# Batch 0 of a fused attention and MLP kernel: a cast split over three engines, W1 pieces paired, a token tile interleaved earlier

## The chip, the cores and the metric

The kernel runs on one core of one Trainium2 chip. The metric is the device time of one execution in microseconds (us), as a median over runs; smaller is better. The core has a matrix engine (TensorE, PE in the profile; its weight loads are listed apart as PEld), a vector engine (VectorE, DVE), a scalar engine for activation functions (ScalarE, ACT), a general engine (GpSimd, POOL) and a queue engine (SyncE, SP). Each runs its own instructions in program order and waits for the others through semaphores. Transfers are issued from the queues of SP, ACT and POOL.

## What is computed

```
x: 8 batches x 8 heads x 512 tokens x 64;  state: 8 x 8 x 32 x 64;  w_in: 512 x 2048;  w_out: 2048 x 512
a     = softmax(x @ state^T / 8)      xread = a @ state      (512 rows per batch)
a2    = softmax(state @ x^T / 8)      sread = a2 @ x         (32 rows per batch)
rows  = [xread, sread] with the 8 heads side by side -> 4352 x 512
out   = silu(rows @ w_in) @ w_out                             (float32)
```

## The kernel before

The kernel never forms xread. For each batch b it multiplies the state by w_in first, which gives a matrix W1 of (8 heads x 32 states) by 2048, held as two groups of 128 rows (`hg` 0 and 1). The hidden layer of the 512 tokens is then silu(aT^T @ W1), where aT is the transposed softmax. The work of a batch is cut as follows.

- A **W1 piece** is 512 columns of W1 of one batch: `w1_mms` (L449) issues 8 matmuls into two PSUM banks, and `w1_out` (L471) copies one bank on DVE and one on ACT into SBUF (`both`, L196). `w1_cols` does both at once. A batch has four pieces.
- A **hidden tile** ft is 128 of the 2048 hidden columns: `emit_G1` (L523) issues two `h` matmuls (one per head group) into one of two PSUM banks of the pool psH and a Silu on ACT (L546) into `g`. `upto(k)` (L592) issues hidden tiles in order until k are done.
- A **step** `G2(b, tt, ft)` (L548) is one `o` matmul: hidden tile ft, token tile tt of 128 tokens, accumulated in an output bank (`o` or `o_a`). Batch 0 has four output banks, o0, o1, a0, a1, for tt = 0 to 3.
- `store` (L564) copies an output bank to SBUF and issues the store on SP.

The attention of a batch is a chain: `cast_x` (L127) turns x into bf16, `pe_transpose_x` (L243) transposes it on PE and copies it out, `scores` (L297) and `exps` (L312) give the exponentials, `norm` (L369) reduces, takes the reciprocal and multiplies (head group 0 on POOL, 1 on DVE), and the result is transposed back (`pe_transpose_a`, L393, as `aT`). ACT loads a function table whenever it goes from Silu to Exp and back; the one-element activations on `warm` (L608, L657, L676) place those loads.

The order on each engine is the order of the program, which is written out by hand. PSUM has eight banks: o0, o1 (psO), two h banks (psH) and a0 to a3 (psA); `bank` hands out the psA banks in turn from the list `banks`. The start of batch 0 (L258 to L270 and L597 to L632) runs its attention chain with x arriving in two transfers, one per head group. In the second head group ACT casts token chunks 2 and 3 and POOL chunks 0 and 1 (L268, L269). Matmuls on zeros (`keep_busy`, L161) fill gaps. W1 of batch 0 starts with 128 and then 384 columns.

The loop L643 goes over hidden tiles 0 to 13 of batch 0: `upto` keeps two to four hidden tiles ahead (LEAD0), at ft = 2, 6, 10 a further W1 piece of batch 0 is made, at ft = 5 and 9 pieces 0 and 1 of batch 1, all in banks a2 and a3; at ft = 4 the state row of batch 1 is transposed, at ft = 11 x of batch 1 is cast, at ft = 12 it is transposed. The fourth token tile (tt = 3) takes part in steps 0 to 2 only. Its steps 3 to 5 come at ft = 12, its steps 6 to 11 while the softmax of batch 1 is on its way, and 12 to 15 after that (L685 to L702), together with pieces 2 and 3 of batch 1. From L704 on, batches 1 to 7 follow in one loop.

Of the kernel before, what the change touches and what calls it, by code (L numbers as in the profile page):

```python
# [9 lines left out]
BF16 = mybir.dt.bfloat16  # L10
# [4 lines left out]
EXP = mybir.ActivationFunctionType.Exp  # L15
# [26 lines left out]
def kernel(  # L42
# [84 lines left out]
    def cast_x(b, eng, c0=0, nc_=4, h0=0, nh=H):  # L127
        if b < 2:
            x_nat[b] = padded(b)
        elif b not in x_nat:  # L130
            x_nat[b] = xpool.tile([128, 4, 4, 128], BF16, tag="x_nat", name=f"x_nat{b}")
        copy(
            eng,
            x_nat[b][:, ds(c0, nc_), ds(h0 // 2, nh // 2), :].rearrange(
                "p c k (u d) -> p c k u d", u=2
            ),
            x_f[b % 2][:, ds(h0, nh), ds(c0, nc_), :].rearrange("p (k u) c d -> p c k u d", u=2),
        )
# [12 lines left out]
    def load_w_out(g0, n):  # L151
        nc.gpsimd.dma_start(w_out_sb[:, ds(g0, n), :], wout_re[:, ds(g0, n), :])

    def copy(eng, dst, src):
        if eng is nc.scalar:
            nc.scalar.activation(dst, src, func=COPY, bias=0.0)  # L156
        else:
            eng.tensor_copy(dst, src)  # L158


    def keep_busy(n, pool, tag):  # L161
        ps = pool.tile([128, 512], FP32, tag=tag, name="ps_busy")
        for _ in range(n):
            nc.tensor.matmul(  # L164
                ps[:], busy[:, 0:128], busy[:], start=True, stop=True, skip_group_check=True
            )
# [50 lines left out]
    def place_one_state(b, ps, eng):  # L217
        for u in range(2):
            by_n = slots_of(b)[u].rearrange("p g (k m v) -> p g k m v", m=16, v=2)
            for v in range(2):  # L220
                copy(eng, by_n[:, :, 0:3:2, :, v], ps[ds(64 * v, 64), :, :, u, :])
# [21 lines left out]
    def pe_transpose_x(b, hg, nb=2, new=bank, engs=(nc.vector, nc.scalar), only=None):  # L243
        if b not in xT:
            xT[b] = xtpool.tile([128, 4, 4, 128], BF16, tag="xT", name=f"xT{b}")
        m = 4 // nb
        for u in range(nb) if only is None else only:
            ps = new([128, m, 2, 128], BF16, "ps_xt")
            for i in range(m):
                for j in range(2):  # L250
                    nc.tensor.transpose(  # L251
                        ps[:, i, j, :],
                        x_nat[b][:, m * u + i, 2 * hg + j, :],
                        ident[:],
                    )
            copy(engs[u], xT[b][:, ds(m * u, m), ds(2 * hg, 2), :], ps[:])
# [9 lines left out]
    o_tags = ["o0", "o1"]  # L266
    new_o = lambda sh, dt, nm: psO.tile(sh, dt, tag=o_tags.pop(), name=nm)
    cast_x(0, nc.scalar, 2, 2, 4, 4)  # L268
    cast_x(0, nc.gpsimd, 0, 2, 4, 4)  # L269
    pe_transpose_x(0, 0, 2, new_o, (nc.vector, nc.vector))  # L270

    st_x = pers.tile([128, 8, B, 4, 2, 2], BF16)

# [116 lines left out]
            aT[b][:, hg, :, :], an[b, hg][:].rearrange("p c s n -> p (c s n)")  # L390
        )

    def pe_transpose_a(b, hg, eng, new=bank, c0=0, n=4):  # L393
        ps = new([128, n, 128], BF16, "ps_at")
        for c in range(n):
            nc.tensor.transpose(ps[:, c, :], an[b, hg][:, c0 + c, :, :], ident[:])
        copy(eng, aT[b][:, hg, ds(c0, n), :], ps[:])


    xm_ps = {}  # L400
# [48 lines left out]
    def w1_mms(b, cols, new=bank):  # L449
        pss = {}  # L450
        if b not in W1:
            W1[b] = wpool.tile([128, 2, DF], BF16, tag="W1", name="W1")
        for f, n in cols:
            for hg in range(2):
                pss[f, hg] = new([128, 512], FP32, "ps_w1")
            for s in range(4):
                for hg in range(2):
                    h = HEAD_OF_SLOT[hg][s]
                    r = 64 * (h % 2)
                    nc.tensor.matmul(  # L460
                        pss[f, hg][ds(32 * s, 32), 0:n],
                        stT[ds(r, 64), b, h // 2, s % 2, :],
                        w_in_sb[ds(r, 64), h // 2, ds(f, n)],
                        start=True,
                        stop=True,
                        tile_position=(r, 32 * s),
                        skip_group_check=True,
                    )
        return pss

    def w1_out(b, cols, engs, pss, at=0):  # L471
        for f, n in cols:
            for hg in range(2):
                copy(engs[hg], W1[b][:, hg, ds(f + at, n)], pss[f, hg][:, ds(at, n)])

    def w1_cols(b, cols, engs, new=bank):
        w1_out(b, cols, engs, w1_mms(b, cols, new))

    def w1_chunks(b, fbs, engs):
        w1_cols(b, [(512 * fb, 512) for fb in fbs], engs)  # L480
# [111 lines left out]
    def upto(k):  # L592
        while done[0] < min(k, (B + 1) * NFT):
            emit_G1(done[0])
            done[0] += 1

    new_h = lambda sh, dt, nm: psH.tile(sh, dt, tag="h1", name=nm)  # L597
    keep_busy(1, psH, "h1")
    scores(0, 0)
    exps(0, 0)  # L600
    keep_busy(1, psH, "h1")
    pe_transpose_x(0, 1, 2, new_h, (nc.vector, nc.scalar))
    norm(0, 0)
    scores(0, 1, 2)
    exps(0, 1)
    norm(0, 1, ((nc.vector, 0, 4),), 2)
    pss0 = w1_mms(0, [(0, 128)])
    nc.scalar.activation(warm[:], busy[:, 0:1], func=SILU, bias=0.0)  # L608
    w1_out(0, [(0, 128)], (nc.scalar, nc.scalar), pss0)
    load_w_in(1024)  # L610
    load_w_out(8, 4)
    load_w_in(1536)
    for hg in range(2):
        load_x(1, 4 * hg, 4)
    load_w_out(12, 4)
    load_states()
    load_x(2)
    for i in range(3):
        ones_beside_x(i, nc.gpsimd)
    keep_busy(3, psH, "h1")  # L620
    pss0 = w1_mms(0, [(128, 384)])
    keep_busy(2, psH, "h1")
    new_o = lambda sh, dt, nm: psO.tile(sh, dt, tag=o_tags.pop(), name=nm)
    o_tags[:] = ["o0", "o1"]
    for c in (0, 2):
        pe_transpose_a(0, 0, nc.scalar, new_o, c, 2)
    for c in (0, 2):
        pe_transpose_a(0, 1, nc.vector, bank, c, 2)
    upto(1)
    w1_out(0, [(128, 128)], (nc.vector, nc.vector), pss0)  # L630
    w1_out(0, [(128, 256)], (nc.vector, nc.vector), pss0, 128)
    upto(2)  # L632

    banks[:] = ["a2", "a3"]
    turn[0] = 0
    W0 = {2: (512, 512), 6: (1024, 512), 10: (1536, 512)}
    LEAD0 = [2, 2, 2, 2, 2, 3, 2, 3, 3, 2, 2, 4, 4]  # L640
    F3 = 3
    ready = 4
    for ft in range(NFT - 2):  # L643
        upto(min(ft + LEAD0[min(ft, 12)], ready))
        if ft in W0:
            w1_cols(0, [W0[ft]], both)
            ready = sum(W0[ft]) // 128
        if ft == 4:
            place_one_state(1, transpose_one_state(st1_n), nc.vector)
        if ft in (5, 9):  # L650
            w1_chunks(1, ({5: 0, 9: 1}[ft],), both)
        if ft == 11:
            for hg in range(2):
                cast_x(1, nc.vector, 0, 4, 4 * hg, 4)
            load_x(3)
        if ft == 12:
            nc.scalar.activation(warm[:], busy[:, 0:1], func=EXP, bias=0.0)  # L657
            for i in range(F3, F3 + 3):
                G2(0, 3, i)
            pe_transpose_x(1, 0, 1, engs=(nc.vector,))  # L660
            pe_transpose_x(1, 1, 1, engs=(nc.vector,))
        for tt in range(4 if ft < F3 else 3):
            G2(0, tt, ft)
    F3 += 3
    banks[:] = ["a2", "a3", "a0", "a1"]
    turn[0] = 0
    scores(1, 0, new=new_h)
    scores(1, 1, new=new_h)
    exps(1, 0)
    exps(1, 1)  # L670
    for tt in (0, 2, 1):
        G2(0, tt, 14)
        G2(0, tt, 15)
        if tt != 1:
            store(0, tt, nc.scalar)
    nc.scalar.activation(warm[:], busy[:, 0:1], func=SILU, bias=0.0)  # L676
    norm(1, 0)
    norm(1, 1, ((nc.vector, 0, 4),))
    tail_tags = ["a2", "a3", "a0", "o0"]

    def tail_bank(shape, dtype, name):
        tag = tail_tags.pop(0)
        return (psO if tag == "o0" else psA).tile(shape, dtype, tag=tag, name=name)

    for ft in range(F3, NFT):  # L685
        if ft == 12:
            pe_transpose_a(1, 0, nc.vector, new_h)
        if ft == 14:
            pe_transpose_a(1, 1, nc.vector, new_h)
            store(0, 1, nc.vector)  # L690
            cols = [(1024, 512), (1536, 512)]
            pss1 = w1_mms(1, cols, tail_bank)
            w1_out(1, cols, (nc.vector, nc.vector), pss1)
            for i in (2, 3):
                for c in range(4):
                    cast_x(i, nc.gpsimd, c, 1)
            transpose_states()
            transpose_x(2)
            upto(NFT + 2)
        G2(0, 3, ft)  # L700
    upto(NFT + 3)
    store(0, 3, nc.vector)  # L702

# [100 lines left out]
```

The softmax here doesn't subtract the row's maximum and nothing guards it: scores larger than these inputs give would overflow.

## Time and profile before

| | us |
|---|---|
| median of 4 runs (lowest, highest) | 216.42 (216.29, 216.45) |
| the profiled execution | 216.29 |
| its span, first to last instruction | 214.5 |
| PE busy in it | 206.0 |
| ACT busy | 139.5 |
| DVE busy | 76.6 |
| POOL busy | 39.4 |

How to read it: the profile is of one execution, whose own time is 1.8 us more than its span. Times inside it are counted from the start of the span. Busy time of PE counts each matmul from its start to its modelled end, and matmuls overlap, so PE is shown busy where it only drains. What tells of idle time on PE is the distance from one start to the next: 0.216 us between matmuls of 512 columns. A few matmul records are missing in a trace, which shows as one distance of about twice that length. In a row of the timeline the number after x is how many instructions were merged into it.

### The profile page before, as it was taken

The numbers are of one execution on the slowest core, as the hardware profiler recorded it, in microseconds if no ns is written. First come the engines' busy times: TensorE is split into PE (matmuls) and PEld (weight loads), VectorE is DVE, ScalarE is ACT, GpSimd is POOL, SyncE is SP. The second block draws the span as 40 slices with busy tenths as digits, with TensorE's granted clock in tenths as the row PEclk, the third lists the DMA queues.
The fourth block names the chain that finished last, engine by engine and source line by source line (L and its number), as shares of the span: only waits on it lengthen the run. The fifth ranks groups of instructions, "written<-read, shape, count | busy, mean of one in ns | idle before, by whom it ended". The sixth has DMA issues, their size and how long they took to land.

```text
span 214.5 us, 3867 instructions
## 1 busy us (share of the span) xinstructions
PE 206.0 (96%) x1549; PEld 96.9 (45%) x1575; DVE 76.6 (36%) x170; ACT 139.5 (65%) x244; POOL 39.4 (18%) x61
## 2 busy tenths in 40 slices
PE   7899999999899999999999999999999999999993
PEld 2443344445344444444444444444444444466653
DVE  3733247855951156106610651135312415200011
ACT  3866577699557876699459956886675366644410
POOL 8683013702420222004110402000200000000000
PEclk9999999999999999999999999999999999999999
DMA  6999999795649447464657395114310211011112
GB/s 185 203 205 207 291 268 349 178 236 205 93 101 271 145 107 196 95 201 105 174 74 244 75 158 121 49 52 104 96 51 18 89 49 53 0 49 49 52 49 98
DMA packets 42914, 28.66 MB, mean 134 GB/s; under 512 B 28048, under 2 KB 37776, under 8 KB 42896
## 3 DMA queue, kind: packets, MB, share of 16 engines
q1 hardware_dynamic: 36720, 20.65, 36.8%
q0 software_dynamic: 5888, 7.64, 17.1%
q8 instruction: 12, 0.20, 0.4%
q10 hardware_dynamic: 288, 0.13, 0.2%
q14 instruction: 6, 0.05, 0.1%
HBM read 17.43 MB, written 8.91 MB: 123 GB/s over the span
## 4 chain that ended last, share of the span: by engine, by line
PE 88%; DVE 5%; ACT 3%; issue 1%; POOL 0%; POOLq 0%
PE o L555 47%; PE h L514 25%; PE ps_w L460 4%; PE h L535 3%; PE o_a L555 2%; PE ps_busy L164 2%; PE o_part L577 2%; DVE W L158 2%; ACT exp_nat L317 1%; DVE rs L376 1%; PE ps_xt L251 1%; PE ps_sr L412 1%; DVE rc L428 1%; PE ps_scT L329 1%; ACT L317 1%
## 5 line engine op out<-in xcount | busy, mean ns | idle before, releaser
L555 PE MATMUL o<-w_out_sb,g 128*128 128x512 bf16 x483 | 129.3, 379 | 1.8 <-issue 1.1
L546 ACT ACTIVATE g<-h 128x512 bf16<-128x512 f32 (+1 forms) x143 | 81.4, 573 | 37.0 <-PE h L514 23.0
L555 PEld LDWEIGHTS <-g 128*128 128x128 bf16 x528 | 50.0, 98 | 57.6 <-issue 3.2
L514 PE MATMUL h<-aT,W 128*128 128x512 bf16 x242 | 72.2, 379 | 0.5 <-ACT g L546 0.3
L158 DVE COPY o_sb<-o 128x512 f32<-128x512 f32 x15 | 10.4, 691 | 89.1 <-PE o L555 85.1
L514 PEld LDWEIGHTS <-W 128*128 128x128 bf16 x254 | 24.5, 98 | 31.8 <-issue 2.0
L158 DVE CAST W<-ps_w 128x512 bf16<-128x512 f32 (+2 forms) x37 | 23.0, 649 | 25.3 <-PE ps_w L460 25.3
L156 ACT ACTIVATE W<-ps_w 128x512 bf16<-128x512 f32 (+1 forms) x31 | 16.4, 570 | 12.6 <-PE ps_w L460 12.6
L158 POOL CAST x_nat<-x_f 128x512 bf16<-128x512 f32 x24 | 14.5, 647 | 33.1 <-issue 22.2
L156 ACT ACTIVATE o_sb<-o 128x512 f32<-128x512 f32 x16 | 9.6, 597 | 12.1 <-PE o L555 8.9
L359 POOL TENSOR_TENSOR an<-e,rcn 128x512 bf16<-128x512 bf16 x5 | 7.6, 1517 | 49.6 <-DVE rcn L357 49.6
L460 PE MATMUL ps_w<-w_in_sb,stT 64*32 64x512 bf16 (+2 forms) x264 | 11.1, 375 | 0.7 <-DVE W L158 0.7
L555 PE MATMUL o_a<-w_out_sb,g 128*128 128x512 bf16 x32 | 10.2, 379 | 0.1
L535 PE MATMUL h<-xmT,w_in_sb 128*128 128x256 bf16 x64 | 9.6, 272 | 0.0
L535 PEld LDWEIGHTS <-w_in_sb 128*128 128x128 bf16 x64 | 6.3, 98 | 3.9
L164 PE MATMUL ps_busy<-busy 128*128 128x512 bf16 x15 | 6.2, 523 | 1.2 <-DVE warm L171 1.2
L460 PEld LDWEIGHTS <-stT 64*32 64x32 bf16 x264 | 3.4, 89 | 7.4 <-issue 4.9
L748 ACT ACT_TABLE_LOAD x5 | 6.4, 1283 | 0.1
L343 ACT ACTIVATE eT<-ps_scT 128x512 bf16<-128x512 f32 x10 | 5.4, 594 | 1.6 <-PE ps_scT L329 1.6
L379 POOL TENSOR_TENSOR an<-exp_nat,rc 128x512 bf16<-128x512 bf16 x3 | 3.1, 1047 | 18.0 <-ACT eT L343 10.7
L356 DVE TENSOR_REDUCE rs<-e 128x32 f32<-128x1024 bf16 x5 | 6.1, 1212 | 0.2 <-DMA e<-eT 0.2
L108 POOL DMA_DIRECT2D x_f<-in_x_dram x4 | 3.3, 845 | 11.7 <-DVE x_rows L158 9.4
(76 smaller groups left out, 104.3 us busy)
## 6 DMA issues: line engine op xcount, KB each, us to landing
out_dram<-o_sb SPq DMA_DIRECT2D x33, 256.0 KB, 2.4
x_f<-in_x_dram SPq DMA_DIRECT2D x4, 1024.0 KB, 6.1
x_f<-in_x_dram POOLq DMA_DIRECT2D x2, 1024.0 KB, 12.7
w_in_sb<-in_moe_w_in_dram POOLq DMA_DIRECT2D x3, 512.0 KB, 10.1
w_out_sb<-in_moe_w_out_dram POOLq DMA_DIRECT2D x3, 512.0 KB, 11.9
x_f<-in_x_dram SPq DMA_DIRECT2D x2, 512.0 KB, 4.8
x_f<-in_x_dram POOLq DMA_DIRECT2D x2, 512.0 KB, 14.8
w_out_sb<-in_moe_w_out_dram POOLq DMA_DIRECT2D x2, 256.0 KB, 8.1
```

Of the source, the lines that this page charges most:

```text
L156: nc.scalar.activation(dst, src, func=COPY, bias=0.0)
L158: eng.tensor_copy(dst, src)
L164: nc.tensor.matmul(ps[:], busy[:, 0:128], busy[:], start=True, stop=True, skip_group_check=True)
L343: nc.scalar.activation(t[:, hg], scT_ps[hg][:], func=EXP, bias=0.0, scale=SCALE)
L356: nc.vector.tensor_reduce(rs[:], e2[b][:], axis=AX, op=ADD)
L359: eng.tensor_tensor(a[:, hg], e2[b][:, hg], rc[:, hg].to_broadcast([128, 4, 4, NS]), op=MULT)
L460: nc.tensor.matmul(pss[f, hg][ds(32 * s, 32), 0:n], stT[ds(r, 64), b, h // 2, s % 2, :], w_in_sb[ds(r, 64), h // 2, ds(f, n)], start=True, ...
L514: nc.tensor.matmul(h_ps[k][:], W1[b][:, hg, ds(128 * ft, 128)], aT[b][:, hg, :, :], start=(hg == 0), stop=(hg == 1), skip_group_check=True,)
L535: nc.tensor.matmul(ps[:, 0:256], w_in_sb[:, kt, ds(128 * ft, 128)], xmT[:, :, kt].rearrange("p t n b -> p t (n b)"), start=(kt == 0), stop ...
L546: nc.scalar.activation(g[:, 0:n], ps[:, 0:n], func=SILU, bias=0.0)
L555: nc.tensor.matmul(outs[tt][:], gt[b * NFT + ft][:, ds(128 * tt, 128)], w_out_sb[:, ft, :], start=(ft == 0), stop=(ft == NFT - 1), skip_gr ...
L748: nc.scalar.activation(warm[:], busy[:, 0:1], func=SILU, bias=0.0)
```

## The change

1. In the cast of the second head group of x of batch 0, POOL keeps chunk 0 and DVE takes chunk 1; ACT keeps 2 and 3. Both copies of the transposed x of that group are DVE's (one was ACT's).
2. The first 128 columns of W1 are copied out on ACT ahead of the load of the Silu table. The transposes of aT of batch 0 use banks o1 and a0 (group 0) and a1 and o0 (group 1); three of the four copies are DVE's, one ACT's. The next 128 columns of W1 are copied by DVE and ACT, not by DVE alone.
3. The state row of batch 1 is transposed at ft = 1.
4. Piece 0 of batch 1 is made at ft = 4. Pieces 1 and 2 are made at ft = 6 and 10, right behind the pieces of batch 0, in the two h banks. Piece 3 stays behind the softmax of batch 1.
5. The fourth token tile runs steps 0 to 6 at ft = 1 to 6 (0 and 1 together), 7 to 11 between the hidden tiles 12 to 15 and the scores of batch 1, and 12 to 15 behind its softmax as before. The loop ends at ft = 11; the steps 12 to 15 of the other three token tiles run together while the softmax is on its way.
6. Hidden tiles 12 to 15 stand around the transposes of x of batch 1. The load of the Exp table follows the last of them.
7. The copy of token tile 1 for its store comes behind the copies of piece 3 on DVE.
8. One W_out load of four row blocks on POOL's queue is split into two.

```diff
     cast_x(0, nc.scalar, 2, 2, 4, 4)
-    cast_x(0, nc.gpsimd, 0, 2, 4, 4)
+    cast_x(0, nc.gpsimd, 0, 1, 4, 4)
     pe_transpose_x(0, 0, 2, new_o, (nc.vector, nc.vector))
+    cast_x(0, nc.vector, 1, 1, 4, 4)
...
-    pe_transpose_x(0, 1, 2, new_h, (nc.vector, nc.scalar))
+    pe_transpose_x(0, 1, 2, new_h, (nc.vector, nc.vector))
...
-    pss0 = w1_mms(0, [(0, 128)])
+    w1_cols(0, [(0, 128)], (nc.scalar, nc.scalar))
     nc.scalar.activation(warm[:], busy[:, 0:1], func=SILU, bias=0.0)
-    w1_out(0, [(0, 128)], (nc.scalar, nc.scalar), pss0)
...
-    load_w_out(12, 4)
+    load_w_out(12, 2)
+    load_w_out(14, 2)
...
     for c in (0, 2):
-        pe_transpose_a(0, 0, nc.scalar, new_o, c, 2)
+        ps_a = (psO, psA)[c // 2].tile(
+            [128, 2, 128], BF16, tag=("o1", "a0")[c // 2], name="ps_at"
+        )
+        at_mms(ps_a, 0, 0, c, 2)
+        copy(both[c // 2], aT[0][:, 0, ds(c, 2), :], ps_a[:])
     for c in (0, 2):
-        pe_transpose_a(0, 1, nc.vector, bank, c, 2)
+        ps_a = (psO, psA)[c == 0].tile(
+            [128, 2, 128], BF16, tag=("o0", "a1")[c == 0], name="ps_at"
+        )
+        at_mms(ps_a, 0, 1, c, 2)
+        copy(nc.vector, aT[0][:, 1, ds(c, 2), :], ps_a[:])
+    w1_out(0, [(128, 128)], both, pss0)
     upto(1)
-    w1_out(0, [(128, 128)], (nc.vector, nc.vector), pss0)
...
     W0 = {2: (512, 512), 6: (1024, 512), 10: (1536, 512)}
-    LEAD0 = [2, 2, 2, 2, 2, 3, 2, 3, 3, 2, 2, 4, 4]
-    F3 = 3
+    W1_AT = {4: 0, 6: 512, 10: 1024}
+    LEAD0 = [2, 2, 2, 2, 2, 3, 2, 1, 3, 3, 2, 1]
+    T3 = {1: (0, 1), 2: (2,), 3: (3,), 4: (4,), 5: (5,), 6: (6,)}
     ready = 4
-    for ft in range(NFT - 2):
-        upto(min(ft + LEAD0[min(ft, 12)], ready))
+    for ft in range(12):
+        upto(min(ft + LEAD0[ft], ready))
+        if ft == 1:
+            place_one_state(1, transpose_one_state(st1_n), nc.vector)
         if ft in W0:
-            w1_cols(0, [W0[ft]], both)
+            pss = w1_mms(0, [W0[ft]])
+            if ft in W1_AT:
+                pss1 = w1_mms(1, [(W1_AT[ft], 512)], new_h)
+            w1_out(0, [W0[ft]], both, pss)
+            if ft in W1_AT:
+                w1_out(1, [(W1_AT[ft], 512)], both, pss1)
             ready = sum(W0[ft]) // 128
-        if ft == 4:
-            place_one_state(1, transpose_one_state(st1_n), nc.vector)
-        if ft in (5, 9):
-            w1_chunks(1, ({5: 0, 9: 1}[ft],), both)
+        elif ft in W1_AT:
+            w1_cols(1, [(W1_AT[ft], 512)], both)
...
-        for tt in range(4 if ft < F3 else 3):
+        for tt in range(3):
             G2(0, tt, ft)
+            if ft == 7 and tt == 0:
+                upto(9)
+        for i in T3.get(ft, ()):
+            G2(0, 3, i)
+    upto(14)
+    G2(0, 3, 7)
+    pe_transpose_x(1, 0, 1, engs=(nc.vector,))
+    upto(15)
+    pe_transpose_x(1, 1, 1, engs=(nc.vector,))
+    upto(16)
+    nc.scalar.activation(warm[:], busy[:, 0:1], func=EXP, bias=0.0)
+    for ft in range(8, 11):
+        G2(0, 3, ft)
     scores(1, 0, new=new_h)
+    G2(0, 3, 11)
     scores(1, 1, new=new_h)
     exps(1, 0)
     exps(1, 1)
-    for tt in (0, 2, 1):
-        G2(0, tt, 14)
-        G2(0, tt, 15)
-        if tt != 1:
-            store(0, tt, nc.scalar)
+    for fts in ((12, 13), (14, 15)):
+        for tt in (0, 2, 1):
+            for ft in fts:
+                G2(0, tt, ft)
+            if fts[1] == 15 and tt != 1:
+                store(0, tt, nc.scalar)
...
+    pe_transpose_a(1, 0, nc.vector, new_h)
+    G2(0, 3, 12)
+    pe_transpose_a(1, 1, nc.vector, new_h)
+    G2(0, 3, 13)
+    banks[:] = ["a2", "a3", "a0", "a1"]
+    turn[0] = 0
+    w1_cols(1, [(1536, 512)], (nc.vector, nc.vector))
+    store(0, 1, nc.vector)
...
+    upto(NFT + 2)
+    G2(0, 3, 14)
+    G2(0, 3, 15)
     upto(NFT + 3)
     store(0, 3, nc.vector)
```

More of the change, by code (lines that the diff above doesn't have):

```diff
@@ L391, in transpose_a, with at_mms, pe_transpose_a @@
         )
-    def pe_transpose_a(b, hg, eng, new=bank, c0=0, n=4):
-        ps = new([128, n, 128], BF16, "ps_at")
+    def at_mms(ps, b, hg, c0=0, n=4):
         for c in range(n):
             nc.tensor.transpose(ps[:, c, :], an[b, hg][:, c0 + c, :, :], ident[:])
-        copy(eng, aT[b][:, hg, ds(c0, n), :], ps[:])
+    def pe_transpose_a(b, hg, eng, new=bank):
+        ps = new([128, 4, 128], BF16, "ps_at")
+        at_mms(ps, b, hg)
+        copy(eng, aT[b][:, hg, :, :], ps[:])
     xm_ps = {}
@@ L597 @@
     new_h = lambda sh, dt, nm: psH.tile(sh, dt, tag="h1", name=nm)
+    new_o = lambda sh, dt, nm: psO.tile(sh, dt, tag=o_tags.pop(), name=nm)
     keep_busy(1, psH, "h1")
@@ L620 @@
     keep_busy(3, psH, "h1")
+    banks[:] = ["a2", "a3"]
+    turn[0] = 0
     pss0 = w1_mms(0, [(128, 384)])
     keep_busy(2, psH, "h1")
-    new_o = lambda sh, dt, nm: psO.tile(sh, dt, tag=o_tags.pop(), name=nm)
-    o_tags[:] = ["o0", "o1"]
     for c in (0, 2):
-        pe_transpose_a(0, 0, nc.scalar, new_o, c, 2)
-    for c in (0, 2):
-        pe_transpose_a(0, 1, nc.vector, bank, c, 2)
+        ps_a = (psO, psA)[c // 2].tile(
[3 more added lines that the diff above has]
+        copy(both[c // 2], aT[0][:, 0, ds(c, 2), :], ps_a[:])
+    for c in (0, 2):
+        ps_a = (psO, psA)[c == 0].tile(
[4 more added lines that the diff above has]
+    w1_out(0, [(128, 128)], both, pss0)
     upto(1)
-    w1_out(0, [(128, 128)], (nc.vector, nc.vector), pss0)
     w1_out(0, [(128, 256)], (nc.vector, nc.vector), pss0, 128)
     upto(2)
-    banks[:] = ["a2", "a3"]
     turn[0] = 0
     W0 = {2: (512, 512), 6: (1024, 512), 10: (1536, 512)}
-    LEAD0 = [2, 2, 2, 2, 2, 3, 2, 3, 3, 2, 2, 4, 4]
-    F3 = 3
+    W1_AT = {4: 0, 6: 512, 10: 1024}
+    LEAD0 = [2, 2, 2, 2, 2, 3, 2, 1, 3, 3, 2, 1]
+    T3 = {1: (0, 1), 2: (2,), 3: (3,), 4: (4,), 5: (5,), 6: (6,)}
     ready = 4
-    for ft in range(NFT - 2):
-        upto(min(ft + LEAD0[min(ft, 12)], ready))
+    for ft in range(12):
+        upto(min(ft + LEAD0[ft], ready))
+        if ft == 1:
+            place_one_state(1, transpose_one_state(st1_n), nc.vector)
         if ft in W0:
-            w1_cols(0, [W0[ft]], both)
+            pss = w1_mms(0, [W0[ft]])
[4 more added lines that the diff above has]
+                w1_out(1, [(W1_AT[ft], 512)], both, pss1)
             ready = sum(W0[ft]) // 128
-        if ft == 4:
-            place_one_state(1, transpose_one_state(st1_n), nc.vector)
-        if ft in (5, 9):
-            w1_chunks(1, ({5: 0, 9: 1}[ft],), both)
+        elif ft in W1_AT:
+            w1_cols(1, [(W1_AT[ft], 512)], both)
         if ft == 11:
@@ L655 @@
             load_x(3)
[L656 to L661, printed above, removed]
-        for tt in range(4 if ft < F3 else 3):
-            G2(0, tt, ft)
-    F3 += 3
-    banks[:] = ["a2", "a3", "a0", "a1"]
-    turn[0] = 0
+        for tt in range(3):
+            G2(0, tt, ft)
+            if ft == 7 and tt == 0:
[11 more added lines that the diff above has]
+        G2(0, 3, ft)
     scores(1, 0, new=new_h)
+    G2(0, 3, 11)
     scores(1, 1, new=new_h)
@@ L678 @@
     norm(1, 1, ((nc.vector, 0, 4),))
[L679 to L700, printed above, removed]
+    pe_transpose_a(1, 0, nc.vector, new_h)
[3 more added lines that the diff above has]
+    banks[:] = ["a2", "a3", "a0", "a1"]
+    turn[0] = 0
+    w1_cols(1, [(1536, 512)], (nc.vector, nc.vector))
+    store(0, 1, nc.vector)
+    for i in (2, 3):
+        for c in range(4):
+            cast_x(i, nc.gpsimd, c, 1)
+    transpose_states()
+    transpose_x(2)
+    upto(NFT + 2)
+    G2(0, 3, 14)
+    G2(0, 3, 15)
     upto(NFT + 3)
```

## The prediction

> **What bounds the kernel now.** I read the page first. In its row of busy times TensorE (PE) leads, and the granted clock is full throughout:
>
> ```profile
> PE 206.0 (96%) x1549; PEld 96.9 (45%) x1575; DVE 76.6 (36%) x170; ACT 139.5 (65%) x244; POOL 39.4 (18%) x61
> ...
> PEclk9999999999999999999999999999999999999999
> ```
>
> 96% can't be read as "no idle": a matmul of 512 columns is listed with 0.38 us, while back to back they start every 0.216 us. So I went to the timeline of PE alone and looked at starts (columns: start, time from first start to last end). All edits lie before 41 us.
>
> ```profile
> 12.90 0.79 PE L555 MATMUL o_a<-w_out_sb,g 128*128 128x512 bf16 x2
> ...
> 20.54 0.38 PE L555 MATMUL o_a<-w_out_sb,g 128*128 128x512 bf16 x1
> 20.97 0.49 PE L460 MATMUL ps_w<-w_in_sb,stT 64*32 64x512 bf16 x8
> 21.39 0.60 PE L555 MATMUL o<-w_out_sb,g 128*128 128x512 bf16 x2
> 21.83 0.38 PE L555 MATMUL o_a<-w_out_sb,g 128*128 128x512 bf16 x1
> 22.26 1.04 PE L514 MATMUL h<-aT,W 128*128 128x512 bf16 x4
> ...
> 27.27 0.38 PE L555 MATMUL o_a<-w_out_sb,g 128*128 128x512 bf16 x1
> 27.70 1.04 PE L514 MATMUL h<-aT,W 128*128 128x512 bf16 x4
> 28.99 0.59 PE L514 MATMUL h<-aT,W 128*128 128x512 bf16 x2 [0.25 <-ACT g L546]
> ```
>
> Two matmuls with 0.79 instead of 0.59 hide a stall of 0.20 (the second o_a needs bank a1, where hidden tile 1 sits until its Silu ends at 13.27). A W1 piece normally begins 0.31 after the last start and gives PE back 0.34 later; at 20.97 it is 0.43 and 0.42, so 0.20 waits for the previous piece's copies out of the same two banks. 21.83 to 22.26 and 27.27 to 27.70 are 0.43 instead of 0.216: 0.21 and 0.22, h waits for DVE's copy of W. 28.99 stands 0.63 after the fourth h (28.36) instead of 0.216: 0.42, h waits for a Silu to free its bank. Sum 1.26 us between 12.0 and 30.1.
>
> Then the timeline of all engines at the hand-over to batch 1:
>
> ```profile
> 30.70 0.60 ACT L546 ACTIVATE g<-h 128x512 bf16<-128x512 f32 x1 [0.48 <-PE h L514]
> ...
> 31.31 1.28 ACT L657 ACT_TABLE_LOAD   x1
> ...
> 33.34 0.63 PE L303 MATMUL ps_sc<-stT,xT 128*128 128x64 bf16 x16
> 33.77 1.09 ACT L317 ACTIVATE exp_nat<-ps_sc 128x512 bf16<-128x512 f32 x2 [0.96 <-PE ps_sc L303]
> ...
> 35.52 1.04 POOL L379 TENSOR_TENSOR an<-exp_nat,rc 128x512 bf16<-128x512 bf16 x1 [5.32 <-DVE rc L377]
> ...
> 36.24 0.88 DVE L379 TENSOR_TENSOR an<-exp_nat,rc 128x512 bf16<-128x512 bf16 x1
> ...
> 36.62 0.40 PE L396 MATMUL ps_at<-ident,an 128*128 128x128 bf16 x4
> ```
>
> The Exp table is in at 32.6 and ScalarE (ACT) waits 0.96 for the scores. From the exps at 33.77, reduce, reciprocal, multiply on POOL and the transposes at 36.62 are one chain that PE can only fill. After it PE is the bound (one h pair and one o every 0.65), so a shift at the first h of batch 1 (38.16) reaches the end whole, if no new wait opens.
>
> **The start.** Here the three-engine cast:
>
> ```profile
> 6.55 0.61 POOL L158 CAST x_rows<-x_f 128x512 bf16<-128x512 f32 x1
> ...
> 7.22 0.62 PE L251 MATMUL ps_xt<-ident,x_rows 128*128 128x128 bf16 x8
> 7.65 0.42 DVE L158 COPY xT<-ps_xt 128x512 bf16<-128x512 bf16 x1 [0.94 <-PE ps_xt L251]
> 7.88 0.60 ACT L156 ACTIVATE xT<-ps_xt 128x512 bf16<-128x512 bf16 x1
> 8.00 0.67 DVE L376 TENSOR_REDUCE rs<-exp_nat 128x16 f32<-128x512 bf16 x1
> ```
>
> POOL's half of 0.61 would end at 6.88; the DVE cast (half of a 0.43 row, about 0.3) lies at 6.64 to 6.93, behind the copies that end at 6.72. PE is streaming the filler of 6.90 until 7.12, so the transposes can come 0.10 earlier at best. Against that a rule speaks: the Trainium skill, GPSIMD Engine Reference, section 1 (Specifications), says GpSimd shares its SBUF interfaces with VectorE and contends with DVE instructions in a two-port mode or with two SBUF inputs. This trace has such a row, the first of POOL's casts of batch 2:
>
> ```profile
> 36.52 1.06 POOL L158 CAST x_nat<-x_f 128x512 bf16<-128x512 f32 x1
> ```
>
> It takes 1.06 where the median of 24 such casts is 0.61, beside the DVE multiply at 36.24, which takes 0.88 where the same one took 0.69 at 10.01. They overlap 0.59 and POOL lost 0.45, three quarters of it. For 0.24 to 0.29 of overlap here that is 0.2: POOL ends near 7.1, the transposes gain 0.05. By the plain row the sum would be 0.05 better. I take the clash.
> The second xT copy moves from ACT to DVE, in front of the reduce: DVE copy 7.60, copy 7.94, reduce about 8.28 instead of 8.00. So both normalised tiles are 0.28 later (POOL's ends 10.44, DVE's 10.99). What absorbs it: before, the aT transposes at 10.97 waited for ACT's W copies, which stood behind a table load (9.26 to 10.54); these copies now go ahead of the load (0.43, 9.15 to 9.6), so the load ends at 10.9, and ACT's one aT copy starts at 11.0, where the first of two started before (10.97). Transposes of the second half group 11.05, DVE copies to 11.85, next DVE W copy to 12.04: the h of tile 1 starts at 12.09 instead of 12.02. Start: +0.07, between 0 and +0.3.
>
> **The stage of PE, 12.1 to the h of hidden tile 15 (before 30.07).** The fourth token tile now has eight steps before that point instead of three: five o matmuls more, 1.08. W1 pieces: before five single ones at 0.44 net each (2.20); after two single and two pairs. A pair costs 0.66: in the tail of before the second of two adjacent pieces starts 0.22 after the first and PE is free 0.33 later. 0.88+1.32 = 2.20, no change. The 16 transposes of x of batch 1 move ahead of that h: 16 x 0.056 = 0.89. All five stalls go (-1.26): the fourth tile starts one step later, when a1 is long free; no piece follows another in the same banks within 2 us; five or six o matmuls (1.1 us or more), not three, cover the copies behind a pair; the h of tiles 12, 13, 14 no longer stand in a row. New waits: the second piece of a pair sits in both h banks and needs the Silus of tiles 6, 7 (10, 11): they end at 21.3, the piece comes at 21.6. Behind it h of tile 8 waits for ACT's second W copy (21.8+0.60+0.55 = 22.95) when PE arrives at 22.97; all of PE queues behind it. I take 0; bounds 0 and 0.6 (one ACT copy later), none below 0, since a wait gives nothing. Tile 15: 30.07+0.07+1.08+0.89-1.26 = 30.85.
>
> **The chain.** Second h 31.07, end 31.45, Silu to 32.08, table load 1.28 to 33.38, exps 0.12 later, 33.50: 0.27 earlier than 33.77. The scores no longer hold it (xT copies end near 31.7). So ACT's table load replaces PE as the late one. POOL's product is ready at 36.30. PE has spent the fourth tile early: twelve o matmuls end near 35.3, then it idles about 1.0 us. That idle costs nothing only because the chain is the path. It should not cost clock either: at the end of the run the granted clock is still 1.00 at 213 us, with the last matmul ending at 211.2 (the table by windows). Behind it: transposes 36.35, one o, transposes at DVE's 36.9, one o, one W1 piece instead of two (-0.22; 0.10 of it lost to waiting for DVE's product): first h of batch 1 at 38.16-0.27-0.12 = 37.77.
>
> **What is moved past queues.** DVE: the store copy of token tile 1 goes behind two W copies: aT to 37.75, W to 39.18, store to 39.8; the first o of batch 1 wants that bank at 39.97. 0.2 of cover. SP: that store is issued about 1.0 later, and with it the state transposes (39.14), xT and the x load behind it; their reader (scores at 48.30) had DVE done at 45.9, so over 1 us is left. POOL: one W_out load becomes two (0.8 us of issue at about 15), the x load of batch 2 waits for a W_in landing at 20.2; the queue still holds bytes until about 27. Batch 1's state row is transposed at 13.6, its load lands at 4.49+8.0 = 12.5. All at 0.
>
> **Sum.** -0.39. The profiled execution took 216.29 (span 214.5), so 215.90; the median of the runs is 216.42, so 216.03. A measurement can tell about 0.2% (0.43 us) from no change.
>
> **Rivals.** A: the start eats it. If POOL stands still and DVE's delay enters whole (+0.35 at the first h) the result is 216.3. For: five DVE steps in a row; against: ACT's table load no longer gates the aT transposes. 0.23. B, slower: the h banks. If ACT's W copies fall behind Silus, each pair stalls PE twice, by 0.3 to 0.6 each; from 0.39 in all the gain is gone, from 0.82 it is slower by 0.2%; at 1.0 it is 217.0. For: margins 0.3 and 0.0; against: ACT has 0.5 of idle there. 0.17. C: no clash and a start 0.1 ahead, each passed on whole: 215.8. 0.12. The forecast, 215.85 to 216.2: 0.48, of which 0.30 below 215.99. Faster 0.30+0.12 = 0.42; same 0.18+0.23 = 0.41; slower 0.17. Range 215.7 to 216.7, which leaves out most of B.
>
> **What would show it.** Right: first h of tile 1 near 12.1; no start-to-start gap over 0.3 between 13 and 30 that isn't a piece; the exps at 33.5 right behind the table load; about 1 us of PE idle before the batch-1 transposes; first h of batch 1 near 37.8. Wrong: h of tile 8 or 12 waiting for W copies, first o of batch 1 waiting for DVE, or scores of batch 2 for the state.

## The result, and the profile after

| | before | after |
|---|---|---|
| median of the runs, us | 216.38 (52 runs, 216.27 to 217.17) | 215.92 (34 runs, 215.76 to 216.26) |
| ratio to before, 95% interval | 1 | 0.998 [0.9975, 0.9984] |
| the profiled execution, us | 216.29 | 216.13 |
| its span, us | 214.5 | 214.3 |

The change gains 0.46 us by the medians, 0.43 by the ratio; 216.03 was forecast. The runs of after lie in two groups of 17, 215.76 to 215.88 and 215.95 to 216.26, so that their median falls into the gap between them; the lower group (median 215.81) stands 0.47 below the 22 lowest runs of before (216.27 to 216.30, median 216.28), and that the moment of the full clock (below) parts the groups is only argued. PE's busy time, the row that led before, hardly moves:

```profile
PE 205.3 (96%) x1549; PEld 97.1 (45%) x1575; DVE 76.7 (36%) x171; ACT 139.3 (65%) x244; POOL 39.9 (19%) x62
```

The two profiled executions differ by 0.16 only, since that of after has a late start (below). So I measure everything from one point, the first h of hidden tile 1, to the first h of batch 1, with the h of tile 15 and the exps of batch 1 between. What lies behind the first h of batch 1 is as long in both, 172.82 us to the last matmul before and 172.83 after; in the eight profiles of the experiments it is 172.83 too. So a shift at this h reaches the end whole. The h of the three landmarks before:

```profile
12.02 0.61 PE L514 MATMUL h<-aT,W 128*128 128x512 bf16 x2
...
30.07 0.59 PE L514 MATMUL h<-aT,W 128*128 128x512 bf16 x2
...
38.16 0.82 PE L514 MATMUL h<-aT,W 128*128 128x512 bf16 x3
```

| us | tile 1 at | tile 1 to tile 15 | to the exps | to first h of batch 1 | sum |
|---|---|---|---|---|---|
| before | 12.02 | 18.05 | 3.70 | 4.39 | 26.14 |
| forecast | 12.09 | 18.76 | 2.65 | 4.27 | 25.68 |
| after | 12.35 | 18.73 | 2.65 | 4.27 | 25.65 |

PE's stage grows by 0.68, the way from tile 15 to the exps shrinks by 1.05, the rest by 0.12: -0.49. The timeline of PE alone, after (start, time from first start to last end):

```profile
12.35 0.60 PE L518 MATMUL h<-aT,W 128*128 128x512 bf16 x2
12.79 0.59 PE L559 MATMUL o<-w_out_sb,g 128*128 128x512 bf16 x2
13.22 0.38 PE L559 MATMUL o_a<-w_out_sb,g 128*128 128x512 bf16 x1
13.44 0.59 PE L518 MATMUL h<-aT,W 128*128 128x512 bf16 x2
...
21.62 0.62 PE L464 MATMUL ps_w<-w_in_sb,stT 64*32 64x512 bf16 x16
22.18 0.60 PE L559 MATMUL o<-w_out_sb,g 128*128 128x512 bf16 x2
22.62 0.59 PE L559 MATMUL o_a<-w_out_sb,g 128*128 128x512 bf16 x2
23.05 0.38 PE L559 MATMUL o<-w_out_sb,g 128*128 128x512 bf16 x1
23.26 0.38 PE L518 MATMUL h<-aT,W 128*128 128x512 bf16 x1
...
28.67 1.03 PE L518 MATMUL h<-aT,W 128*128 128x512 bf16 x4
29.54 0.38 PE L559 MATMUL o_a<-w_out_sb,g 128*128 128x512 bf16 x1
29.75 0.61 PE L251 MATMUL ps_xt<-ident,x_rows 128*128 128x128 bf16 x8
...
31.08 0.59 PE L518 MATMUL h<-aT,W 128*128 128x512 bf16 x2
...
35.00 0.59 PE L559 MATMUL o<-w_out_sb,g 128*128 128x512 bf16 x2
36.56 0.40 PE L396 MATMUL ps_at<-ident,an 128*128 128x128 bf16 x4 [0.97 <-POOL an L380]
```

The 0.79 behind tile 1 (before, at 12.90) is a 0.59 (12.79) and the next starts follow every 0.216. A pair of pieces (21.62) begins 0.31 behind the last start and gives PE back at 22.18, and h of tile 8 (23.26) comes 0.21 behind the o ahead of it. That is the place where the slower rival would have shown, and it had nothing to spare: ACT's copy that frees the h bank ends at 23.20, 0.06 ahead of this h, and in e9 (below), where h waits for that copy, it also starts 0.06 behind it. The h at 28.67 stands right behind an o, and the Silu stall of before 28.99 is gone. At 35.0 PE has nothing left: the next start would be at 35.43, the transposes come at 36.56, 1.13 of idle.

The timeline of all engines over the same hand-over:

```profile
31.71 0.60 ACT L550 ACTIVATE g<-h 128x512 bf16<-128x512 f32 x1 [0.28 <-PE h L518]
...
32.16 0.40 PE L304 MATMUL ps_sc<-stT,xT 128*128 128x64 bf16 x8
32.32 1.28 ACT L686 ACT_TABLE_LOAD   x1
...
33.73 1.06 ACT L318 ACTIVATE exp_nat<-ps_sc 128x512 bf16<-128x512 f32 x2
...
35.46 1.04 POOL L380 TENSOR_TENSOR an<-exp_nat,rc 128x512 bf16<-128x512 bf16 x1 [4.50 <-ACT o_sb L156]
...
38.00 1.04 PE L518 MATMUL h<-aT,W 128*128 128x512 bf16 x4
...
39.33 0.68 DVE L158 COPY o_sb<-o 128x512 f32<-128x512 f32 x1
...
40.20 0.38 PE L559 MATMUL o<-w_out_sb,g 128*128 128x512 bf16 x1
```

Silu, table load and exps now stand end to end; the 0.96 that ACT waited for the scores before is gone, because the scores (32.16) run under the table load. The late store copy on DVE ends at 40.0 and the first o of batch 1 starts at 40.20, 2.20 behind the first h, as before (2.21). The state transposes on SP are issued at 40.42 (before 39.14); the unchanged 172.83 behind the first h shows no wait for them.

The late start is visible on PE and DVE. A row of before, then rows of after from 5 us on:

```profile
5.53 0.62 PE L251 MATMUL ps_xt<-ident,x_rows 128*128 128x128 bf16 x8
```

```profile
5.51 1.04 PE L251 MATMUL ps_xt<-ident,x_rows 128*128 128x128 bf16 x8
...
6.34 0.57 PE L164 MATMUL ps_busy<-busy 128*128 128x512 bf16 x1
...
6.52 0.44 POOL L158 CAST x_rows<-x_f 128x256 bf16<-128x256 f32 x1
...
6.92 0.28 DVE L158 CAST x_rows<-x_f 128x256 bf16<-128x256 f32 x1
```

Eight transposes take 1.04 from 5.51 where before they took 0.62 from 5.53, and a filler 0.57 where it takes 0.38. The transposes start 0.107 apart instead of 0.056, about half as fast. The trace's record of the granted clock begins, with the full clock, at 6.71 us here and at 5.35 in the profile of before; the windows and the row PEclk show full also ahead of that, where nothing is recorded. The Trainium skill, TensorE: Matmul & The Clock Gate (Part 1), gives 106.7 and 55.6 ns between starts for the half and the full clock, and the starts here agree. It puts the change at about 4 us of sustained matmuls, give or take 0.5 us from run to run; in the ten profiles of this case it comes between 3.88 and 7.11 us, which is 2.7 to 5.9 us behind the first filler at 1.19, so it varies more than that. It is a matter of the execution, not of the change, as experiment e5 shows.

### The profile page after: what moved, and what is told of

It is laid out like the page before. It is cut to its first block, busy times and chain, and to the rows that moved or that the text cites. A ratio compares the mean times of both kernels' runs of the same rounds, so it can differ in the third digit from the quotient of the medians.

```text
span 214.3 us, 3868 instructions
## 1 busy us (share of the span) xinstructions
PE 205.3 (96%) x1549; PEld 97.1 (45%) x1575; DVE 76.7 (36%) x171; ACT 139.3 (65%) x244; POOL 39.9 (19%) x62
## 4 chain that ended last, share of the span: by engine, by line
PE 86%; DVE 4%; DMA 4%; ACT 3%; issue 1%; POOL 1%; POOLq 0%
PE o L559 47%; PE h L518 25%; PE ps_w L464 4%; DMA w_in_sb<-in_moe_w_in_dram 4%; PE h L539 3%; PE o_a L559 2%; PE o_part L581 2%; DVE W L158 1%; PE ps_sr L416 1%; DVE rc L432 1%; ACT exp_nat L318 1%; PE ps_scT L330 1%; ACT L318 1%; ACT L686 1%; DVE rs L377 1%
## 5 line engine op out<-in xcount | busy, mean ns | idle before, releaser
L158 DVE CAST W<-ps_w 128x512 bf16<-128x512 f32 (+2 forms) x35 | 22.1, 659 | 26.4 <-PE ps_w L464 26.4
L156 ACT ACTIVATE W<-ps_w 128x512 bf16<-128x512 f32 (+1 forms) x33 | 17.1, 562 | 12.6 <-PE ps_w L464 12.6
L559 PE MATMUL o_a<-w_out_sb,g 128*128 128x512 bf16 x30 | 9.6, 379 | 0.0
L432 DVE RECIPROCAL rc<-ps_sr 32x2 f32<-32x2 f32 x32 | 5.2, 164 | 0.3
```

Source lines behind the costliest of these rows:

```text
L432: nc.vector.reciprocal(rc[q, :], src)
L559: nc.tensor.matmul(outs[tt][:], gt[b * NFT + ft][:, ds(128 * tt, 128)], w_out_sb[:, ft, :], start=(ft == 0), stop=(ft == NFT - 1), skip_gr ...
```

## Theory and rivals, and the experiments

**Theory.** The gain comes from the head of batch 1's softmax chain. The change costs PE time ahead of tile 15, and gets it back by taking scores and transposes out from between the Silu and the exps. The start gives nothing. **Rival 1:** the start gives part of the gain (or takes part of it). **Rival 2:** the fourth tile's early steps give it, by closing stalls. **Rival 3:** PE's work is what counts everywhere, so that the 1.13 idle shows no slack. A consequence of the theory: a step of the fourth tile ahead of tile 15 costs its 0.216 whole, and behind the exps it costs nothing while there is idle left; so the change does too much too early.

e1, e2, e3 and e5 ran on one chip beside 37 runs of before with a median of 216.44; e4, e6, e7 and e9 on another beside 29 runs with a median of 216.63, 7 of which took 217.76 to 217.9. So the times expected for these four, which were worked out from 216.4, have to be read about 0.2 higher, and where the intervals of the ratio are too wide, the distances from tile 1 decide.

**e1_start_alone.** In the kernel before, parts 1 and 2 of the change only (casts, copies of xT, copies of the first W1 columns, banks of aT):

```diff
-    cast_x(0, nc.gpsimd, 0, 2, 4, 4)
+    cast_x(0, nc.gpsimd, 0, 1, 4, 4)
     pe_transpose_x(0, 0, 2, new_o, (nc.vector, nc.vector))
+    cast_x(0, nc.vector, 1, 1, 4, 4)
...
-    pe_transpose_x(0, 1, 2, new_h, (nc.vector, nc.scalar))
+    pe_transpose_x(0, 1, 2, new_h, (nc.vector, nc.vector))
...
```

> The kernel before with the changed start alone (cast of three engines, both xT copies on DVE, first W1 columns copied ahead of the table load, new banks for aT). My theory: the start is no gain; the first h of hidden tile 1 comes 0 to 0.1 us later than before at the same clock, total within 0.1 us of the kernel before (216.4 +- 0.1). Rival: the start is where the gain comes from, then 215.9.

Measured: 216.51 (13 runs, 216.28 to 216.93), ratio 1.0004 [0.9996, 1.0012]. From tile 1 to the first h of batch 1 26.14, as before. The start gives nothing that these runs can tell. Its profile is that of its slowest run, and its tile 1 at 12.65 tells nothing of the change: x came 0.22 later than in the profile of before (5.26, 5.04), and DVE's first cast, which the change doesn't touch, took nearly double (0.43 in before):

```profile
5.26 0.81 DVE L158 CAST x_rows<-x_f 128x512 bf16<-128x512 f32 x1 [1.27 <-DMA x_f<-in_x_dram]
```

**e2_old_start.** The kernel after, with parts 1 and 2 undone, the copies and banks of part 2 too:

```diff
-    cast_x(0, nc.gpsimd, 0, 1, 4, 4)
+    cast_x(0, nc.gpsimd, 0, 2, 4, 4)
     pe_transpose_x(0, 0, 2, new_o, (nc.vector, nc.vector))
-    cast_x(0, nc.vector, 1, 1, 4, 4)
...
```

> The changed kernel with the start of the kernel before. My theory: the gain stays or grows by up to 0.1 us, 215.8 to 215.95. Rival (the gain comes from the start): 216.4.

Measured: 215.94 (19 runs), ratio 0.9985 [0.9974, 0.9995]; the distance is 37.72-12.07 = 25.65, that of after. All of the gain is there without the new start. Rival 1 falls from both sides.

**e3_fill4.** The kernel after with four matmuls on zeros (0.86 us of PE) in the idle time ahead of the transposes of batch 1; the fillers are work that nobody reads:

```diff
+    keep_busy(4, psH, "h1")
     norm(1, 0)
```

> The changed kernel with four matmuls on zeros (4 x 0.216 = 0.86 us) put on PE between the twelve o matmuls and the transposes of the normalised tile of batch 1. My theory: PE is idle there for 1.1 us and waits for the softmax chain, so this costs nothing: 215.9. Rival (PE itself is the path at this place): +0.86, 216.8.

Measured: 215.94 (11 runs, 215.78 to 216.12), ratio 0.998 [0.9971, 0.9988], equal to after. PE's timeline:

```profile
34.95 0.59 PE L559 MATMUL o<-w_out_sb,g 128*128 128x512 bf16 x2
35.38 1.03 PE L164 MATMUL ps_busy<-busy 128*128 128x512 bf16 x4
36.52 0.40 PE L396 MATMUL ps_at<-ident,an 128*128 128x128 bf16 x4
...
37.95 1.04 PE L518 MATMUL h<-aT,W 128*128 128x512 bf16 x4
```

Four matmuls more, and the transposes come 2.84 behind the exps (33.68), as they do in after (36.56-33.73 = 2.83).

**e4_fill10.** The same with ten (2.16 us of PE).

```diff
+    keep_busy(10, psH, "h1")
     norm(1, 0)
```

> The changed kernel with ten matmuls on zeros (10 x 0.216 = 2.16 us) in the idle stretch in place of four. My theory: the first 1.1 us are free and the rest is paid in full: +1.0 us over the changed kernel, 216.9. Rival (the stretch is not idle but slack that later work absorbs): under 216.3.

Measured: 217.07 (12 runs), ratio 1.0026 [1.0005, 1.0047].

```profile
35.54 2.32 PE L164 MATMUL ps_busy<-busy 128*128 128x512 bf16 x9
37.70 0.39 PE L396 MATMUL ps_at<-ident,an 128*128 128x128 bf16 x4
...
39.01 1.04 PE L518 MATMUL h<-aT,W 128*128 128x512 bf16 x4
```

(One of the ten records is missing.) The distance is 39.01-12.46 = 26.55, 0.91 more than in after. 2.16 less the idle of 1.13 would be 1.03; 0.1 comes back because the transposes of the second head group no longer wait for DVE's product. So the idle has an edge where the rows put it: below it PE work is free, above it each matmul counts. Rival 3 falls.

**e5_four_steps_later.** The kernel after with four steps of the fourth tile fewer ahead of tile 15 and four more behind the exps:

```diff
-    T3 = {1: (0, 1), 2: (2,), 3: (3,), 4: (4,), 5: (5,), 6: (6,)}
+    T3 = {1: (0, 1), 2: (2,), 6: (3,)}
...
     upto(14)
-    G2(0, 3, 7)
...
-    for ft in range(8, 11):
+    for ft in range(4, 7):
         G2(0, 3, ft)
     scores(1, 0, new=new_h)
-    G2(0, 3, 11)
+    G2(0, 3, 7)
...
+    for ft in range(8, 12):
+        G2(0, 3, ft)
     nc.scalar.activation(warm[:], busy[:, 0:1], func=SILU, bias=0.0)
     norm(1, 0)
```

> The changed kernel with four of the eight fourth-tile steps that run ahead of hidden tile 15 put behind it: steps 3, 4, 5 out of the loop and the one step between hidden tile 13 and the transposes; four steps then fill the idle stretch behind the twelve o matmuls. My theory: the path runs from the h of hidden tile 15 over Silu, table load, exps and softmax, so everything behind comes 4 x 0.216 = 0.86 us earlier and the idle stretch shrinks from 1.1 to 0.3 us: 215.05. Rival (arrival of x of batch 1, its casts on DVE or W loads hold the hand-over): no gain, 215.9; a rival in which the missing cover behind a W1 piece brings stalls back: 215.4 to 215.6.

Measured: 215.13 (5 runs, 215.0 to 215.35), ratio 0.9942 [0.993, 0.9955]: faster than both kernels, by 1.3 us than before and 0.8 than after. PE's timeline:

```profile
30.27 0.59 PE L518 MATMUL h<-aT,W 128*128 128x512 bf16 x2
...
34.62 1.03 PE L559 MATMUL o_a<-w_out_sb,g 128*128 128x512 bf16 x4
35.77 0.40 PE L396 MATMUL ps_at<-ident,an 128*128 128x128 bf16 x4
...
37.20 1.04 PE L518 MATMUL h<-aT,W 128*128 128x512 bf16 x4
```

The four o matmuls at 34.62 lie where after idles; 0.28 of idle is left (35.77-34.62-4x0.216). From tile 15 to the exps 2.65 and from there to the first h 4.27, both as in after: the whole gain is ahead of tile 15, where it was expected. The stage is 18.25 instead of 18.73, only 0.48 less, since this execution has a stall that after's profile does not have:

```profile
18.04 0.41 PE L464 MATMUL ps_w<-w_in_sb,stT 64*32 64x512 bf16 x8
18.78 0.59 PE L559 MATMUL o<-w_out_sb,g 128*128 128x512 bf16 x2 [0.33 <-ACT g L550]
```

PE came 0.74 behind the start of the piece instead of 0.35: 0.39. The row names a Silu; what came last was the W_out load with the row blocks of this step, of whose 16 parts the last landed at 18.74 and the others by 17.06 (all by 17.2 to 17.9 in the other profiles). The Silu can't have been it: it belongs to the next hidden tile, and in e9 it runs at 18.15 as here, while this step starts at 18.38. Without the stall the gain over after is 0.48+0.39 = 0.87, four times 0.216. The start tells of the clock too, in the timeline of all engines:

```profile
5.50 0.62 PE L251 MATMUL ps_xt<-ident,x_rows 128*128 128x128 bf16 x8
...
6.53 0.44 POOL L158 CAST x_rows<-x_f 128x256 bf16<-128x256 f32 x1
6.60 0.52 DVE L158 CAST x_rows<-x_f 128x256 bf16<-128x256 f32 x1
...
7.09 0.61 PE L251 MATMUL ps_xt<-ident,x_rows 128*128 128x128 bf16 x8
```

Here the clock is full at 5.41, about as in before, and with the start of the change tile 1 stands at 12.02: the same as before. With the clock full at 3.88 (e9) it is 12.02 as well, and the old start with the clock full at 4.05 (e2) gives 12.07. At equal clock the new start is worth 0.00 to 0.05.

**e6_fourth_alone.** In the kernel before, only the fourth tile's steps 0 to 6 spread over ft = 1 to 6:

```diff
-    F3 = 3
+    F3 = 7
+    T3 = {1: (0, 1), 2: (2,), 3: (3,), 4: (4,), 5: (5,), 6: (6,)}
...
-        for tt in range(4 if ft < F3 else 3):
+        for tt in range(3):
             G2(0, tt, ft)
+        for i in T3.get(ft, ()):
+            G2(0, 3, i)
```

> The kernel before with the fourth token tile interleaved as in the change (steps 0 to 6 at hidden tiles 1 to 6), and nothing else changed. My theory: four more o matmuls stand ahead of the hand-over (+0.86 us), the wait for bank a1 goes (-0.20), and one more o covers part of the waits behind the W1 pieces (about -0.4), while PE then idles behind the hand-over: slower by 0.2 to 0.4 us, 216.6 to 216.8. Rival (the interleaving is what gains): 216.0.

Measured: 216.74 (12 runs), ratio 1.0003 [0.9986, 1.0019], which tells nothing. The distances tell: 38.91-12.52 = 26.40, 0.26 more than before, all of it between tile 1 and tile 15 (18.30 against 18.05). What it moved left a hole where the work was before:

```profile
35.84 0.59 PE L555 MATMUL o_a<-w_out_sb,g 128*128 128x512 bf16 x2
37.37 0.40 PE L396 MATMUL ps_at<-ident,an 128*128 128x128 bf16 x4 [0.93 <-POOL an L379]
```

Four o matmuls more ahead of tile 15 are 0.86, of which closed stalls give 0.61 back. ACT still waits 0.96 for the scores, as in before and in e1. Alone, the earlier fourth tile is a loss of 0.26. Rival 2 falls.

**e7_no_pairs.** The kernel after with piece 1 of batch 1 alone at ft = 8 and piece 2 back behind the softmax, next to piece 3:

```diff
-    W1_AT = {4: 0, 6: 512, 10: 1024}
+    W1_AT = {4: 0, 8: 512}
...
-    w1_cols(1, [(1536, 512)], (nc.vector, nc.vector))
     store(0, 1, nc.vector)
...
+    w1_cols(1, [(1024, 512), (1536, 512)], (nc.vector, nc.vector), tail_bank)
```

(`tail_bank` hands out a2, a3, a0 and o0.)

> The changed kernel without pairs: the piece of columns 512 of batch 1 goes alone to hidden tile 8 (banks a2, a3), the piece of columns 1024 goes back behind the softmax of batch 1 next to the last one, with the store copy of token tile 1 ahead of their copies. My theory: ahead of hidden tile 15 the same PE time (five single pieces at 0.44 = 2.20, as two singles and two pairs), behind the softmax one more piece, +0.22: 216.1 to 216.2. Rival (the pairs in the h banks are what removes the stalls): back to 216.4.

Measured: 216.37 (12 runs), ratio 0.9986 [0.9967, 1.0006], again too wide. The distance is 38.29-12.41 = 25.88, 0.23 more than in after. The stage to tile 15 is 18.75, after's 18.73: five single pieces cost PE there what six cost in after, four of them in pairs. So pairs close no stall, and what they give is the sixth piece, which else stands behind the softmax: there 0.21 of the 0.23 lies, with two pieces in front of the first h:

```profile
37.73 0.62 PE L464 MATMUL ps_w<-w_in_sb,stT 64*32 64x512 bf16 x16
38.29 0.82 PE L518 MATMUL h<-aT,W 128*128 128x512 bf16 x3
```

**e9_six_steps_later.** e5 with two more steps moved behind the exps:

```diff
-    T3 = {1: (0, 1), 2: (2,), 6: (3,)}
+    T3 = {1: (0, 1)}
...
-    for ft in range(4, 7):
+    for ft in range(2, 5):
         G2(0, 3, ft)
...
-    G2(0, 3, 7)
+    G2(0, 3, 5)
...
-    for ft in range(8, 12):
+    for ft in range(6, 12):
```

> As the run with four steps later, but steps 2 and 3 go behind hidden tile 15 as well, so that no fourth-tile step stands behind a W1 piece. My theory: each of the two o matmuls taken away opens a wait of 0.2 us for the copies of the piece, and the idle stretch had only 0.3 us left: no gain over the four-step version, 215.1 to 215.3. Rival (only the number of steps ahead of tile 15 counts): 214.7 to 214.85.

Measured: 215.18 (6 runs), ratio 0.9934 [0.9915, 0.9953]; not told apart from e5. The stage to tile 15 takes 17.87, e5 without its stall 17.86. The two matmuls fewer (0.43) were given back to two waits that they had covered:

```profile
15.99 0.38 PE L559 MATMUL o_a<-w_out_sb,g 128*128 128x512 bf16 x1
16.65 0.38 PE L518 MATMUL h<-aT,W 128*128 128x512 bf16 x1 [0.28 <-ACT W L156]
```

A hidden tile has two h; the row at 16.65 is the second of its tile, since the next o follows at 16.87, and the record of the first is missing. One distance ahead of it puts the first at 16.43: 0.44 behind the o instead of 0.216, right behind the copies of the W1 piece, which end at 16.37 on DVE and 16.39 on ACT. The second wait stands behind the pair: h of tile 8 comes 0.43 behind its o (21.86 to 22.29), with one o fewer between, and 0.06 behind ACT's copy. The two waits are 0.22 and 0.21, as much as the two matmuls. So some steps of the fourth tile are needed early, as cover for the piece copies, and the edge lies near e5.

No run moves the scores and the transposes of x alone. That they are the gain is read from the rows (ACT's wait of 0.96 for the scores is there in before, e1 and e6, and in none of the other seven profiles) and from what is left when the start (e1, e2), the fourth tile (e6) and the pairs (e7) are taken one by one.

## Why the prediction was right, step by step

- **PE's stage** (18.76 forecast, 18.73 measured): five o more, 16 transposes, 1.26 of stalls away, six pieces, four of them in pairs, at the price of five. e7 confirms the last term (18.75 with five single ones).
- **Chain, table load in place of PE** (2.65 and 2.65), **behind the exps** (4.27 and 4.27), with piece 2 worth 0.22: right. Putting it back in e7 costs 0.21 there.
- **The idle of 1.0 us is free**: 1.13 measured, free by e3, with its edge shown by e4.
- **The start** is the term that was mis-sized: "Start: +0.07, between 0 and +0.3", measured 0.00 at equal clock (12.02 in e5 and e9 against 12.02 before). In e5 the second transposes stand at 7.09, 0.13 ahead of before, where 0.05 was forecast, and both normalised tiles are 0.19 later, not 0.28; at tile 1 that came out even. POOL's half of the cast takes two thirds of the whole one's 0.61, not half, which "would end at 6.88" had passed over.
- **The clash of POOL and DVE** in that term was wrong in kind: the prediction let POOL pay for it. In e5 and e9 the two casts overlap by 0.35 or more, and DVE's takes 0.52 and 0.51; in after, e1, e3, e4 and e7, where they overlap by 0.13 at most, it takes 0.28. POOL's takes 0.44 in after as well, with 0.04 of overlap, so its 0.44 and 0.45 in e5 and e9, against 0.40 elsewhere, are not the clash. The rule of the Trainium skill, GPSIMD Engine Reference, section 1 (Specifications), fits these rows, though no trace shows which mode DVE's cast runs in. Who loses, in these rows, is the engine that starts second. Here POOL starts first, by 0.08 and 0.10, and DVE ends 0.16 behind POOL's end. In the row from which the price was taken DVE's multiply came first and POOL's cast ended 0.47 behind it, as in e5, where it overlaps less and takes 0.86. In e9 the two do not overlap, and each of POOL's four casts takes 0.61:

```profile
34.27 1.04 POOL L380 TENSOR_TENSOR an<-exp_nat,rc 128x512 bf16<-128x512 bf16 x1 [3.71 <-ACT o_sb L156]
...
34.99 0.87 DVE L380 TENSOR_TENSOR an<-exp_nat,rc 128x512 bf16<-128x512 bf16 x1
...
36.02 2.28 POOL L158 CAST x_nat<-x_f 128x512 bf16<-128x512 f32 x4 [0.70 <-DMA x_f<-in_x_dram]
```

DVE's multiply takes 0.87 here all the same, so its 0.88 before was not the price of POOL's cast. It overlaps POOL's own multiply, and in all ten profiles, in batch 0 and batch 1, it ends 0.54 to 0.55 behind that one's end, taking 0.70 with 0.15 of overlap and 0.88 with 0.33.

- **Rival A** (the start eats the gain) is false: e2. **Rival B** (h banks stall behind pairs) is false: 23.26 stands 0.21 behind its o. The margin was the 0.0 that the prediction gave, as the 0.06 behind ACT's copy shows, and in e9 one o fewer opens the wait; the bounds 0 and 0.6 were fair. **Rival C** (the start a gain of 0.1 and no clash) is false as well. The median is 0.11 below the forecast: 0.07 is the change's own (-0.46 by the medians where -0.39 was forecast), which is the size of the start's term; 0.04 is the median of before, 216.38 in 52 runs where it was 216.42 in four. That the medians fit so closely is in part luck, since that of after falls into a gap; the lowest runs of both kernels give -0.47.
- **Queues**: DVE's late store copy, SP's late transposes (1.28 later, where about 1.0 was forecast) and POOL's split load cost nothing that the trace of after shows. In e5 a W_out load was late once; it is the load of row blocks 4 to 7, not the one that was split, and whether the split has a part in that was not tried.
- **The clock**: "full throughout" was read from a row that has no record ahead of 5.35. Ahead of it the fillers of before start 0.40 to 0.43 apart, not 0.216. That the moment of the full clock moves from run to run, and tile 1 with it by 0.3 to 0.4, is not among the terms of the prediction.

## What to carry to other kernels

When a serial chain (softmax, table load) hands over to a stage that PE bounds, look for the instruction that heads the chain: PE work ahead of it is paid in full, PE work behind it is free up to the chain's idle, so move independent work behind the head until that idle is full and no further. Pulling work forward to close stalls ahead of the head pays only where the stall is longer than the work; leave just the matmuls there that cover a copy. For effects of 0.2 us compare distances between two landmarks within one profile, since the start alone moves a run by as much. And where VectorE and GpSimd meet, look at which of them starts first.

## What was not expected of the hardware

- The granted clock became full between 3.88 and 7.11 us in ten profiles of nearly the same start. With the new start, late release goes with a late tile 1: its h at 12.30 and 12.41 with 6.25 and 6.29 (e3, e7), at 12.35 with 6.71 and at 12.46 with 7.11 (e4), against 12.02 with 5.41 and with 3.88.
- The same DVE cast of x took 0.43 in eight profiles, 0.81 in e1 and 0.70 in e6, though none of the kernels changes it. In these two x landed later, so that the cast started at 5.26 and 5.38 instead of 5.01 to 5.20, well behind the start of POOL's DMA issue (5.02), and it ended 0.25 behind the end of that issue (5.82) in both. That is the pattern of the multiplies, second starter behind first; as the cause it is only argued, and why x landed late stays open.
- Where instructions of VectorE and GpSimd overlapped, the one that started second lost time: POOL's cast behind DVE's multiply 0.45 and 0.25 us with 0.59 and 0.39 of overlap (before, e5), DVE's cast behind POOL's 0.24 and 0.23 with 0.36 and 0.35 (e5, e9).
- A W_out load landed between 17.2 and 18.74 us, and in e5 that was a stall of 0.39.
